# Own PSUM tiles in place of shared pairs, and four weight slots in place of three, in a spectral mixer with a gated feed-forward

## The chip, the cores and the metric

The kernel runs on one core of one Trainium2 chip. The metric is the device time of one execution in microseconds. The engines' names in profile lines: PE is the matrix engine (PEld its weight loads), DVE the vector engine, ACT the scalar engine, POOL the GpSimd engine, SP the engine that issues all DMAs of this kernel.

## What is computed

A token matrix `x` of 8192 x 448 goes through two residual branches, both modulated by a condition vector `c`:

```python
mod = silu(c) @ w_mod                      # six rows: sa, ca, ga, sb, cb, gb
h = layernorm(x) * (1 + ca) + sa
x = x + ga * A(h)                          # spectral part
h = layernorm(x) * (1 + cb) + sb
x = x + gb * ((gelu(h @ w_gate) * (h @ w_up)) @ w_down)     # feed-forward part

def A(h):                                  # per 4 blocks of 112 channels
    z = rfft(h, over the 8192 tokens)      # complex
    h1 = relu(z @ w1 + b1)                 # complex product, relu on both parts
    o = h1 @ w2 + b2                       # complex product
    o = softshrink(o, 0.01)
    return irfft(o)
```

`w_gate` and `w_up` are 448 x 1792, `w_down` is 1792 x 448. All inputs and outputs are float32.

## The kernel before

**Spectral part.** The transform over 8192 = 128 x 64 tokens is done in two stages of matrix products. A first stage loads `x`, takes the statistics of its rows and makes the 128-point transform (`dft_a`, `out_a`), storing its result `td` in DRAM. Then 32 *units* (16 groups of frequencies `bt`, two halves `h` of the channels) run through a software pipeline. `step(i)` works on several units at once: it fetches unit i+2 (`fetch_t`), makes the 64-point transform of unit i (`stage_s2`, tag `pa`), splits unit i+1 into a high and a low half-precision part (`split_t`), makes the second product of the block MLP with softshrink for unit i-2 (`stage_m2`, two halves p, tag `pc`), the first part of the inverse transform for unit i-3 (`stage_i1`, tag `pd`), and the first MLP product for unit i-1 (`stage_m1`, tag `pb`). Each of these writes PSUM with PE, reads it back with ACT and then DVE (a high part and the remainder), and calls `bank(tag, ...)` twice a unit, once for each half of its work. `drain` ends the pipeline.

Between the stages of a step stand *hooks* (`load`, `pe`, `act`, `dve`, `pool`): work of the feed-forward part that is done early. In steps 3 to 16 that is the norms of the weights (`squares`, `norms`, `down_max`, `down_sums`); in steps 17 to 31 the weights are turned into *forms*, sums and differences of weight blocks in two half-precision parts (`load_forms`, `form_sums`, `forms_hi`, `forms_lo`, `store_forms`), and the down weights are made ready (`load_d4`, `down_hi`, `down_lo`). A form is the weight operand of one of seven column groups t; it takes 23 blocks of 128 columns, `NWB`, in two precisions, and is kept in DRAM (`wsd`) in the parts that `WPARTS` lists.

**Feed-forward part.** The tokens are worked through in 32 chunks of 2 x 128. Per chunk there are 7 *periods*, one for each form, and then the down products:

- `period(u)` runs the gate and up products of form `torder[u]` in four groups of matmuls, `stage_a` and `stage_b` for u, `stage_c` for u-1, `stage_d` for u-2, into `sets[u % 3]`, a tile of two PSUM banks, with the reads by ACT and DVE (`seed`, `copy_b`, `joins`, `gel3`, `mult3`, `gel1`, `mult1`), sums on POOL (`sums`) and the split into two precisions (`quant_hi`, `quant_lo`) between them. `torder` runs through the seven forms forwards in one chunk and backwards in the next, so the forms still held in a slot at the turn aren't fetched again.
- after period `LA` = 2 of a chunk `phase` runs: the second stage of the inverse transform for chunk i+2 (`inverse`, `residual`), and then `down` for chunk i-1, which makes seven products (numbered 0 to 6) of 7 x 3 matmuls each. They go to `d0`, `d1` (the two banks of `pd`) and `f0`, `f1` (the two banks of the set that is free). Its last step stores the output.
- `extra` and `first` (for the first chunk) list what else is done at the end of a period: the split of the inverse transform's inputs (`split_v`, `split_g`), the token operand's sums and packing into `pkt` (`token_sums`, `pack_hi`, `pack_lo`) and its transposition by DMA into `nt` (`transposes`, 12 DMAs of 4 blocks a chunk).

The forms live in slots of SBUF: two that the spectral part fills, and one more. `plan_slots` gives each u a slot, taking the one whose last use is longest ago, and notes in `refill` which u is to be fetched into it. `after(u, part)` issues this fetch right where the slot's part was used last.

**What sets the order.** The program's order is the order on each engine (`manual_schedule`); the framework adds the waits, by tiles. All DMAs are issued by SP in program order, and a DMA that waits holds those behind it.

Of the kernel before, what the change touches and what calls it, by code (L numbers as in the profile page):

```python
# [19 lines left out]
D = 448  # L20
# [3 lines left out]
HC = 224  # L24
# [11 lines left out]
WPARTS = (12, 11)  # L36
# [11 lines left out]
def spectral_geglu(ctx, tc, x, w1, b1, w2, b2, wg, wu, wd, cvec, wmod, cf1, cs2, cmi, cgm, out):  # L48
# [26 lines left out]
    ident = cpool.tile([128, 128], F16, name="ident")  # L75
    make_identity(nc, ident)
# [249 lines left out]
    with ExitStack() as bctx:  # L326
# [593 lines left out]

        def load_g(i):
# [64 lines left out]
        at(31, "load", load_g, 0)  # L986
        at(31, "load", load_v0)
# [7 lines left out]

    with ExitStack() as cctx:
        cp = cctx.enter_context(tc.tile_pool(name="cp", bufs=1, side="right"))
        wslot.append(cp.tile([128, 2, NWB, 128], F16, name="ws2"))
        nch = NB // CB
        NT_ = nch * NP  # L1000
        sets = [banks2[tag] for tag in ("pa", "pb", "pc")]
        pdn = banks2["pd"]
# [6 lines left out]
        def plan_slots():  # L1009

            held = [[0 if wat[0] == s else 1, -1] for s in range(2)] + [[2, -1]]
# [11 lines left out]
        def load_part(u, part):  # L1023

            a, n = (0, WPARTS[0]), WPARTS
            lo = a[part]
            dma(slot_of[u][:, :, lo : lo + n[part]], wsd[part][torder[u]])

        def after(u, part):

            if u in refill:
                load_part(refill[u], part)
# [109 lines left out]
        def transposes(i, gs):  # L1142
            if i not in nts:
                nts[i] = cp.tile([128, 2, NXT, 128], F16, tag="nt", name="nt", bufs=2)
            for g in gs:
                sw_, c = divmod(g, NXT // 4)
                o = 64 * sw_ + 512 * c
                nc.sync.dma_start(nts[i][:, sw_, 4 * c : 4 * c + 4, :], pkt[:, o : o + 512], transpose=True)  # L1148
# [79 lines left out]
        def gel1(u):  # L1228
            gls[u] = cp.tile([128, 128], F32, tag="gl1", name="gl1", bufs=2)
# [39 lines left out]
        def down(i, pf, mid=lambda n: None):  # L1269
# [13 lines left out]
            d0, d1, f0, f1 = (p[:, b, :] for p in (pdn, pf) for b in range(2))  # L1283
            heads = [(0, d0), (1, d1)] + ([(2, f0), (4, f1)] if last else [])
# [16 lines left out]
            V.tensor_tensor(u2, product(i, f1, 4, rest if last else range(NP)), p1, ALU.add)  # L1301
            V.tensor_tensor(u4, product(i, d0, 3), u2, ALU.add)  # L1302
# [226 lines left out]
```

## Time and profile before

| | us |
|---|---|
| median of 3 runs | 2530.32 (2530.08 to 2536.79) |
| the profiled execution | 2528.75 |
| its span, first to last instruction | 2526.9 |

| part of the span | us from its start |
|---|---|
| first `stage_s2` matmul starts | 82.2 |
| last `stage_i1` first matmul starts | 777.6 |
| first `gel3` of the feed-forward part starts | 824.6 |
| end | 2526.9 |

How to read the lines that follow: a group's line holds the source line, engine, operation, `output<-inputs` by the program's tile names, shapes and count, then busy time and mean duration of one in ns, then the idle time of the engine ahead of it and who ended it (`<-`). A line of the table of waits holds engine and line, the releaser, the total in us, the number of times and the longest. A line of the timeline holds start and duration in us, engine, line, operation, count, and in brackets the idle time before. "issue" is time in which an engine waited for nothing that the profile shows. Matmuls overlap in the pipeline and their ends are modelled, so distances between starts say more than durations.

### The profile page before, as it was taken

Reading aid. Unit: us, or ns where it says so; the run is one execution under the profiler, and the core shown is the slowest. Engines: PE = TensorE matmul, PEld = TensorE weight load, DVE = VectorE, ACT = ScalarE, POOL = GpSimd, SP = SyncE. Lnnn points to the kernel's source line nnn. Section 1 sums busy time; section 2 is a strip of 40 time slices with the busy share of each in tenths; the row PEclk is TensorE's granted clock in tenths of the full one; section 3 lists DMA queues with packets and bytes.
Section 4 is the critical chain, followed back from the end, with each engine's and each line's share of the span. In section 5 each row is a group of like instructions: output and inputs, shape, how many; then the busy total and the mean of one; then the engine's idle time right before and its main releaser. Section 6 shows DMA issues by size and latency. Waiting matters only on the chain.

```text
span 2526.9 us, 92738 instructions
## 1 busy us (share of the span) xinstructions
PE 2034.0 (80%) x41348; PEld 1893.0 (75%) x41348; DVE 1459.9 (58%) x2958; ACT 1047.3 (41%) x1917; POOL 1107.1 (44%) x1531
## 2 busy tenths in 40 slices
PE   7676676655655798889888988989898898898898
PEld 3565666555554788888888888988888888888887
DVE  8423323444444576676666766767666766677644
ACT  6333333344431444443344443444334444344442
POOL 3122323232210555455455554655545555555532
PEclk9757657777777999999999999999999999999999
DMA  9643433335335977667866687666776766777562
GB/s 351 210 136 95 123 87 89 100 104 153 102 97 150 191 178 192 156 162 180 177 177 185 160 184 175 180 182 160 187 164 168 190 159 162 189 175 196 142 162 82
DMA packets 378984, 405.18 MB, mean 160 GB/s; under 512 B 223700, under 2 KB 287320, under 8 KB 378584
## 3 DMA queue, kind: packets, MB, share of 16 engines
q1 hardware_dynamic: 378584, 399.26, 60.9%
q8 instruction: 323, 5.29, 0.9%
q14 instruction: 77, 0.63, 0.1%
HBM read 290.96 MB, written 57.80 MB: 138 GB/s over the span
## 4 chain that ended last, share of the span: by engine, by line
PE 67%; DVE 13%; issue 7%; ACT 7%; DMA 3%; SPq 2%; POOL 1%; ACTq 0%; DVEq 0%; POOLq 0%
PE pb L1164 11%; PE pa L1164 11%; PE pc L1164 11%; PE pd L1264 4%; PE pd L1266 3%; PE pd L1265 3%; DVE y L470 2%; SPq L1148 1%; DVE x L1226 1%; ACT t L462 1%; PE pc L448 1%; PE pb L421 1%; PE pa L375 1%; ACT th L112 1%; DVE c L1210 1%
## 5 line engine op out<-in xcount | busy, mean ns | idle before, releaser
L1164 PEld LDWEIGHTS <-ws 64*128 64x128 f16 x33600 | 965.7, 95 | 197.6 <-issue 186.2
L1164 PE MATMUL pa<-nt,ws 64*128 64x128 f16 x11250 | 384.4, 219 | 64.0 <-issue 37.0
L1164 PE MATMUL pb<-nt,ws 64*128 64x128 f16 x11250 | 386.7, 219 | 51.5 <-issue 40.7
L1164 PE MATMUL pc<-nt,ws 64*128 64x128 f16 x11100 | 379.9, 218 | 50.4 <-issue 38.3
L1254 DVE SCALAR_TENSOR_TENSOR ac<-x,sa_act,ac 128x896 f16<-128x896 f32 x224 | 317.8, 1419 | 19.8 <-ACT ac L1245 19.8
L1222 ACT ACTIVATE gl<-c,dg 128x384 f32<-128x384 f32 x224 | 138.0, 616 | 400.8 <-DVE c L1216 385.8
L1264 PE MATMUL pd<-wd,ac 128*128 128x224 f16 x896 | 233.3, 260 | 30.2 <-DVE u L1302 15.4
L1266 PE MATMUL pd<-wd,ac 128*128 128x224 f16 x896 | 232.7, 260 | 1.8 <-DVE ac L1254 1.0
L1265 PE MATMUL pd<-wd,ac 128*128 128x224 f16 x896 | 232.7, 260 | 0.8 <-issue 0.8
L1245 ACT ACTIVATE ac<-x,sa_act 128x896 f16<-128x896 f32 x224 | 231.2, 1032 | 0.6 <-DVE x L1240 0.4
L1237 POOL TENSOR_TENSOR x<-x 128x128 f32<-128x128 f32 x223 | 105.6, 474 | 271.6 <-DVE x L1226 271.6
L470 DVE SCALAR_TENSOR_TENSOR y<-pc,t 64x224 f32<-64x224 f32 x256 | 99.5, 389 | 187.4 <-ACT t L462 184.8
L1226 DVE TENSOR_TENSOR x<-c,gl 128x384 f32<-128x384 f32 x224 | 181.6, 811 | 31.0 <-ACT gl L1222 31.0
L1265 PEld LDWEIGHTS <-ac 128*128 128x128 f16 x1568 | 153.6, 98 | 59.8 <-issue 59.6
L114 POOL TENSOR_TENSOR yl<-y,yh 128x448 fp32r<-128x448 f32 x63 | 73.7, 1170 | 268.8 <-ACT yh L112 268.8
L1308 POOL TENSOR_TENSOR o<-u,p 128x224 f32<-128x224 f32 x32 | 21.1, 659 | 383.8 <-DVE u L1307 383.8
L1264 PEld LDWEIGHTS <-ac 128*128 128x128 f16 x1568 | 153.6, 98 | 9.0 <-issue 7.9
L114 POOL TENSOR_TENSOR tl<-tr,th 128x896 f16<-128x896 f32 x30 | 56.5, 1883 | 227.4 <-ACT th L112 174.6
L1266 PEld LDWEIGHTS <-ac 128*128 128x128 f16 x1568 | 153.5, 98 | 2.7 <-DVE ac L1254 1.3
L448 PE MATMUL pc<-w2h,hh 113*128 113x224 f32 x128 | 52.6, 411 | 112.6 <-DVE y L470 112.6
L1240 POOL TENSOR_TENSOR x<-x 128x128 f32<-128x128 f32 x223 | 129.2, 579 | 19.2 <-DVE x L1233 18.9
L439 DVE SCALAR_TENSOR_TENSOR hl<-pb,hh 112x512 fp32r<-112x512 f32 x60 | 41.5, 692 | 144.5 <-ACT hh L438 144.3
(345 smaller groups left out, 4636.1 us busy)
## 6 DMA issues: line engine op xcount, KB each, us to landing
ws<-wsd SPq DMA_DIRECT2D x129, 768.0 KB, 5.9
ws<-wsd SPq DMA_DIRECT2D x129, 704.0 KB, 5.3
tr<-td SPq DMA_DIRECT2D x64, 224.0 KB, 4.0
vd<-us SPq DMA_DIRECT2D x64, 224.0 KB, 2.9
xx<-in_A_x SPq DMA_DIRECT2D x32, 448.0 KB, 4.3
v<-vd SPq DMA_DIRECT2D x63, 224.0 KB, 2.8
out<-x SPq DMA_DIRECT2D x31, 448.0 KB, 2.7
xt<-in_A_x SPq DMA_DIRECT2D x15, 896.0 KB, 13.2
```

The costliest lines, as they stand in the source:

```text
L114: (el or V).tensor_tensor(lo, src, h, ALU.subtract)
L470: V.scalar_tensor_tensor(y[ri * 64 : ri * 64 + 64, gi], pv[si, ri], LAM, tv[si, ri], op0=ALU.add, op1=ALU.min)
L1164: T.matmul(ps2[:, pr, reg * 128 : reg * 128 + 128], slot[rows, hl, wb + j, :], xblock(i, pr, xb + xo + j), start=start and j == 0 and m == ...
L1222: S.activation(gls[u], cts[u][:, 0], AF.Gelu_apprx_tanh, scale=dg)
L1226: V.tensor_tensor(xs[u][:, 1::3, :], cts.pop(u)[:, 1], gls.pop(u), ALU.mult)
L1237: e.tensor_tensor(s1, a21, a22, ALU.add)
L1240: e.tensor_tensor(s4, a12, s2, ALU.subtract)
L1245: S.activation(acts[u][:, 0], xs[u][:, 0:7], AF.Copy, scale=sa_act[:, t : t + 1])
L1254: V.scalar_tensor_tensor(acts[u][:, 1], xs.pop(u)[:, 0:7], sa_act[:, t : t + 1], acts[u][:, 0], op0=ALU.mult, op1=ALU.subtract)
L1264: T.matmul(ps, ac[:, 0, ka], w[:, 0, kb], start=n == 0, stop=False)
L1265: T.matmul(ps, ac[:, 0, ka], w[:, 1, kb], start=False, stop=False)
L1266: T.matmul(ps, ac[:, 1, ka], w[:, 0, kb], start=False, stop=n == NP - 1)
```

## The change

**PSUM.** In the spectral part the four tiles of two banks each (`banks2`, alternated by `turn`) become a pool of one-bank tiles: each call of `bank` takes a new tile, two buffers for each tag. That pool is closed before the feed-forward part, which opens another: three tiles of two banks as `sets`, and two tiles of one bank as `pdn`. In `down` product 4 now goes to `d0` and product 3 to `f1` (they were the other way round), and of the last chunk's products three in place of four are begun early.

**Slots.** There are four slots of forms, in three parts of 12, 6 and 5 blocks. `after` only notes a fetch in `pending`; `flush` issues what is noted, at the end of each period, ahead of that period's `extra`. To find the room in SBUF `gl1` has one buffer in place of two, and an identity that isn't used is no longer made.

**Order of the other DMAs.** `load_g(i+2)` moves from `phase` of the chunk before to the end of period 0, `load_v(i+3)` to the end of period 6, `split_v` from period 0 to period 1. The twelve transposes, which stood in periods 1 and 2 (4 and 8), are now spread over periods 1 to 4 (2, 6, 2, 2); those of the first two chunks take 12 blocks each in place of 4. The load of the modulation row `gb` moves from the feed-forward part's start into the last units of the spectral part.

```diff
-WPARTS = (12, 11)
+WPARTS = (12, 6, 5)
...
-    psum = ctx.enter_context(tc.tile_pool(name="psum", bufs=1, space=bass.MemoryType.PSUM))
-    banks2 = {tag: psum.tile([128, 2, 512], F32, name=tag) for tag in ("pa", "pb", "pc", "pd")}
-    turn = dict.fromkeys(banks2, 0)
+    pctx = ExitStack()
+    psum = pctx.enter_context(tc.tile_pool(name="psum", bufs=2, space=bass.MemoryType.PSUM))
 
     def bank(tag, name):
-        turn[tag] += 1
-        return banks2[tag][:, turn[tag] % 2, :]
+        return psum.tile([128, 512], F32, tag=tag, name=name)
...
+        def load_gb():
+
+            raw = fp.tile([128, 14, 128], F32, tag="wr", name="wr", bufs=2).rearrange("p k f -> p (k f)")
+            raws["gb"] = [raw[:112, h * 896 : (h + 1) * 896].rearrange("p (q c) -> p q c", q=4) for h in range(2)]
+            for h in range(2):
+                c0 = 5 * D + h * HC
+                dma(raws["gb"][h], wmod[:, c0 : c0 + HC].rearrange("(k p) c -> p k c", p=112))
...
+        at(31, "load", load_gb)
...
+    pctx.close()
...
-        wslot.append(cp.tile([128, 2, NWB, 128], F16, name="ws2"))
+        wslot += [cp.tile([128, 2, NWB, 128], F16, name=f"ws{s}") for s in (2, 3)]
...
-        sets = [banks2[tag] for tag in ("pa", "pb", "pc")]
-        pdn = banks2["pd"]
+        psum2 = cctx.enter_context(tc.tile_pool(name="psum2", bufs=1, space=bass.MemoryType.PSUM))
+        sets = [psum2.tile([128, 2, 512], F32, name=f"set{s}") for s in range(3)]
+        pdn = [psum2.tile([128, 512], F32, name=f"pdn{s}") for s in range(2)]
...
-                    s = min(range(3), key=lambda n: held[n][1])
+                    s = min(range(4), key=lambda n: held[n][1])
...
+        pending = []
+
         def after(u, part):
 
             if u in refill:
-                load_part(refill[u], part)
+                pending.append((refill[u], part))
+
+        def flush(keep=()):
+
+            for u, part in [p for p in pending if p[1] not in keep]:
+                load_part(u, part)
+                pending.remove((u, part))
...
-            gls[u] = cp.tile([128, 128], F32, tag="gl1", name="gl1", bufs=2)
+            gls[u] = cp.tile([128, 128], F32, tag="gl1", name="gl1")
...
-            d0, d1, f0, f1 = (p[:, b, :] for p in (pdn, pf) for b in range(2))
-            heads = [(0, d0), (1, d1)] + ([(2, f0), (4, f1)] if last else [])
+            (d0, d1), (f0, f1) = pdn, (pf[:, b, :] for b in range(2))
+            heads = [(0, d0), (1, d1)] + ([(2, f0)] if last else [])
...
-            V.tensor_tensor(u2, product(i, f1, 4, rest if last else range(NP)), p1, ALU.add)
-            V.tensor_tensor(u4, product(i, d0, 3), u2, ALU.add)
+            V.tensor_tensor(u2, product(i, d0, 4), p1, ALU.add)
+            V.tensor_tensor(u4, product(i, f1, 3), u2, ALU.add)
...
             on(u - 2, stage_d)
-            on(u - 2, lambda v: after(v, 1))
+            on(u - 2, lambda v: after(v, 2))
...
             on(u - 1, stage_c)
+            on(u - 1, lambda v: after(v, 1))
...
-                loads(j + 1)
...
         extra = {
-            0: [(2, split_v)],
-            1: [(2, split_g), (1, transposes, range(0, 4))],
-            2: [(1, transposes, range(4, 12))],
-            3: [(2, token_sums, 0), (2, pack_hi, [0]), (2, pack_lo, [0])],
-            4: [(2, token_sums, 1), (2, pack_hi, [1]), (2, pack_lo, [1])],
+            0: [(2, load_g)],
+            1: [(2, split_v), (2, split_g), (1, transposes, [0, 6])],
+            2: [(1, transposes, [1, 7, 11, 5, 2, 8])],
+            3: [(1, transposes, [3, 9]), (2, token_sums, 0), (2, pack_hi, [0]), (2, pack_lo, [0])],
+            4: [(1, transposes, [4, 10]), (2, token_sums, 1), (2, pack_hi, [1]), (2, pack_lo, [1])],
             5: [(2, pack_hi, [2]), (2, pack_lo, [2])],
-            6: [(2, pack_hi, [3]), (2, pack_lo, [3])],
+            6: [(2, pack_hi, [3]), (2, pack_lo, [3]), (3, load_v)],
         }
...
-            if i < nch and k == LA and i > 0:
-                for d, fn, *args in extra[k]:
-                    if i + d > 1 and i + d < nch:
-                        fn(i + d, *args)
+            if i == nch:
+                continue
+            flush()
+            for d, fn, *args in extra[k]:
+                if i + d > (1 if fn is transposes else 2) and i + d < nch:
+                    fn(i + d, *args)
+            if k == LA and i > 0:
                 phase(i)
-            elif i < nch:
-                for d, fn, *args in extra[k]:
-                    if i + d > (1 if fn is transposes else 2) and i + d < nch:
-                        fn(i + d, *args)
```

More of the change, by code (lines that the diff above doesn't have):

```diff
@@ L7 @@
 from concourse import mybir
-from concourse.masks import make_identity
 from concourse._compat import with_exitstack
@@ L1009, in plan_slots @@
         def plan_slots():
-            held = [[0 if wat[0] == s else 1, -1] for s in range(2)] + [[2, -1]]
+            held = [[0 if wat[0] == s else 1, -1] for s in range(2)] + [[2, -1], [3, -1]]
             for u, t in enumerate(torder):
@@ L1341, in loads @@
         def loads(j):
-            if j < nch:
-                load_v(j)
-                load_g(j)
+            load_v(j)
+            load_g(j)
         def phase(i):
@@ L1387, in spectral_geglu @@
         }
-        inverse(0, banks2["pa"], halves[0])
-        ga, gb = nxt[0]["ga"], bank("pd", "psm")
+        inverse(0, sets[0], halves[0])
+        ga, gb = pdn
         mod_half("ga", ga, 1)
@@ L1394, in spectral_geglu @@
         S.copy(ga_r[:, HC:], ga[:, HC:D])
[L1395 to L1400 removed]
+        inverse(0, sets[1], halves[1])
         for h in range(2):
@@ L1409, in spectral_geglu @@
         loads(1)
-        for part in range(2):
+        for part in range(len(WPARTS)):
             load_part(2, part)
@@ L1423, in spectral_geglu @@
         S.copy(gb_r, gb[:, :D])
-        transposes(0, range(12))
-        inverse(1, banks2["pb"])
+        transposes(0, range(4), 12)
+        for part in range(len(WPARTS)):
+            load_part(3, part)
+        inverse(1, sets[2])
         residual(1)
```

25 lines of the change are left out of this document (8 added, 17 removed).

## The prediction, made before the changed kernel was run

> **What bounds the kernel now.** I read the page first (sums, the slices, the chain that ended last), then windows cut at the program's own steps, then the table of waits and the timeline.
>
> ```profile
> span 2526.9 us, 92738 instructions
> ...
> PE 2034.0 (80%) x41348; PEld 1893.0 (75%) x41348; DVE 1459.9 (58%) x2958; ACT 1047.3 (41%) x1917; POOL 1107.1 (44%) x1531
> ...
> PEclk9757657777777999999999999999999999999999
> ...
> q8 instruction: 323, 5.29, 0.9%
> ...
> PE 67%; DVE 13%; issue 7%; ACT 7%; DMA 3%; SPq 2%; POOL 1%; ACTq 0%; DVEq 0%; POOLq 0%
> ```
>
> TensorE carries two thirds of the last chain. The clock row splits the span: about 0.7 of full speed over the first third (the spectral part), full speed afterwards (the feed-forward part). The next fence cuts the spectral part into its first five steps, steps 5 to 16, steps 17 to 30, and the rest; columns after the length are busy time of PE, PEld, DVE, ACT, POOL, then granted clock, DMA share, GB/s. The two rows below it are the same cuts for L375 alone, which issues 8 matmuls a step, so 96 and 112 are 12 and 14 steps.
>
> ```profile
> 82.00:159.00 77.00, 50.17 (x307) 45.70 (x307) 23.88 (x43) 25.41 (x42) 14.35 (x10) 0.66 0.57 176
> 159.00:417.40 258.40, 179.76 (x1073) 163.17 (x1072) 86.87 (x195) 91.90 (x149) 75.91 (x104) 0.66 0.35 99
> 417.40:725.20 307.80, 184.46 (x1097) 165.61 (x1096) 130.35 (x218) 121.59 (x186) 95.31 (x77) 0.72 0.44 117
> 725.20:778.30 53.10, 35.56 (x178) 31.49 (x177) 19.14 (x35) 17.65 (x30) 5.66 (x5) 0.74 0.19 51
> ```
>
> ```profile
> 159.00:417.40 258.40, 25.42 (x96) 17.18 (x96) 0.66 0.35 99
> 417.40:725.20 307.80, 23.99 (x112) 17.22 (x113) 0.72 0.44 117
> ```
>
> A step lasts 258.4/12 = 21.5 us in the first cut ("A") and 307.8/14 = 22.0 us in the second ("B"). In A it holds 15.0 us of PE, 7.2 of DVE, 7.7 of ACT, 6.3 of POOL and 0.35 x 21.5 = 7.5 us of DMA: nothing is full. In B: PE 13.2, DVE 9.3, ACT 8.7, POOL 6.8, DMA 9.7. What fills the rest are waits of PE:
>
> ```profile
> PE pc L448 <- DVE y L470: 112.6, 32, 6.1
> ...
> PE pb L421 <- DVE hl L439: 53.0, 28, 4.1
> ...
> PE pa L375 <- DVE zl L384: 45.5, 29, 1.6
> ...
> PE pd L500 <- ACT us L504: 19.9, 32, 0.7
> ```
>
> ```profile
> 361.06 0.41 PE L453 MATMUL pc<-w2h,hl 112*128 112x224 f32 x1
> 361.57 0.63 ACT L462 ACTIVATE t<-pc,nlam 128x448 f32<-128x448 f32 x1 [0.23 <-PE pc L453]
> 362.31 1.60 DVE L470 SCALAR_TENSOR_TENSOR y<-pc,t 64x224 f32<-64x224 f32 x4 [1.97 <-ACT t L462]
> 364.05 0.52 PE L448 MATMUL pc<-w2h,hh 113*128 113x224 f32 x1 [2.58 <-DVE y L470]
> ```
>
> The matmul at 364.05 writes the *other* half of `pc` than the one ACT and DVE are reading (`bank` alternates the index), yet it starts 0.14 us after the last read. So the two banks of one tile exclude each other, although nothing is shared. The four rows are this wait in four places, about once a step each: 231.0 us, 7.2 us a step. Two different tiles don't do this: here PE writes `pc` while ACT reads `pb`.
>
> ```profile
> 1212.12 0.85 PE L1164 MATMUL pc<-nt,ws 64*128 64x128 f16 x24
> 1212.34 0.58 ACT L1201 COPY sb<-pb 128x512 f32<-128x512 f32 x1 [0.19 <-PE pb L1164]
> ```
>
> **The change, part by part.**
>
> **1. Spectral part: each call gets its own one-bank tile, two per tag.** The 7.2 us a step go; a tile then waits only for the readers of its predecessor but one, which finished a step ago. What is late next? The clock matters too:
>
> ```profile
> 755.11 0.41 PE L453 MATMUL pc<-w2h,hl 112*128 112x224 f32 x1
> 755.32 0.41 PE L448 MATMUL pc<-w2h,hh 113*128 113x224 f32 x1
> ...
> 755.86 0.27 PE L451 MATMUL pc<-w2h,hh 112*128 112x224 f32 x1
> 755.97 0.27 PE L452 MATMUL pc<-w2l,hh 112*128 112x224 f32 x1
> ```
>
> The same matmul starts every 0.21 us, then every 0.11: half clock and full clock. PE's 15.0 us a step in A, at the granted 0.66, are 15.0 x 0.66 = 9.9 us at full clock; B's are 13.2 x 0.72 = 9.5. [...]
>
> Upper bound of a new step: only the idle goes, 21.5 - 7.2 = 14.3 (A) and 22.0 - 7.2 = 14.8 (B). Lower bound: the fullest resource, PE's 9.9 (A) and the DMA's 9.7 (B). A dependent loop remains, since the second MLP product of a step needs `hl` of the step before:
>
> ```profile
> L439 DVE SCALAR_TENSOR_TENSOR hl<-pb,hh 112x512 fp32r<-112x512 f32 x60 | 41.5, 692 | 144.5 <-ACT hh L438 144.3
> ```
>
> Six matmuls twice at 0.11 (1.3), relu 0.63, two `y` of 1.60, `hl` twice 0.69: 6.5 us, in B plus the weight-form work that sits ahead of `hl` on DVE (9.3 - 7.2 = 2.1 more). Both lie under the lower bounds, so I stay nearer to those: 11 us in A, 13 in B (four resources between 8.7 and 9.7 in order there, so more is lost between them). A: 258.4 - 132 = **-126** (bounds -87 to -140). B: 307.8 - 182 = **-126** (-101 to -172). The five first steps fill the pipeline beside a DMA that is busy 0.57 x 77 = 44 us: 77 to 57, **-20** (0 to -33). The drain has the same waits: **-10** (0 to -15).
>
> **2. Feed-forward part: `pd` becomes two tiles, and products 3 and 4 change places.** The down products show the same exclusion, three times a chunk, 32 chunks:
>
> ```profile
> 1200.50 0.26 PE L1265 MATMUL pb<-wd,ac 128*128 128x224 f16 x1
> 1200.59 0.26 PE L1266 MATMUL pb<-wd,ac 128*128 128x224 f16 x1
> 1201.29 0.26 PE L1264 MATMUL pb<-wd,ac 128*128 128x224 f16 x1 [0.43 <-ACT p L1298]
> ```
>
> ```profile
> PE pd L1264 <- DVE u L1302: 15.4, 32, 0.5
> PE pd L1264 <- ACT p L1292: 13.9, 32, 0.4
> ...
> PE pb L1264 <- ACT p L1298: 4.8, 11, 0.4
> ```
>
> Starts are 0.70 apart in place of 0.10, so 0.60 is lost where the idle column says 0.43: 0.17 more each. A chunk loses 0.48 + 0.43 + 0.43 + 3 x 0.17 = 1.85 us. After: product 1 goes to a tile of its own; product 4, on `pdn[0]`, stands between the two that share a tile, and its 21 matmuls at 0.10 cover the copy (0.43); product 5 has its own tile. 32 x 1.85 = **-59** (-40 to -59; PE is on the chain here). The last product keeps its real wait. With one head fewer in the last chunk at most 18 matmuls, 1.7 us, lose their cover: within rounding.
>
> **3. Four slots, three parts, flushed at the end of a period.** By the slot plan 3 forms a chunk are fetched in place of 4: of the 129 issues below some 98 stay.
>
> ```profile
> ws<-wsd SPq DMA_DIRECT2D x129, 768.0 KB, 5.9
> ```
>
> PE hardly ever waits for weights, so this is not where they cost. The instruction queue is: 5.29 MB for 2 x 41348 instructions are 64 B each, 323 packets of 256 instructions, and PE stops between such packets when other transfers run:
>
> ```profile
> 1219.00:1228.00 9.00, 4.60 (x160) 4.26 (x156) 6.35 (x11) 3.28 (x6) 5.01 (x10) 1.00 0.85 310
> 1228.00:1238.00 10.00, 9.83 (x354) 9.66 (x350) 5.43 (x10) 7.79 (x14) 5.74 (x10) 1.00 0.02 6
> ```
>
> ```profile
> PEld L1164 <- issue: 186.2, 205, 11.8
> ```
>
> At 310 GB/s PE is busy 4.60 of 9.00 us, at 6 GB/s 9.83 of 10.00. The 186.2 us (waits for nothing shown) are my bound for all such stops. Traffic beside the gate/up products per chunk now: three of four forms (4.4 MB at 768 + 704 KB), inputs and output (1.5), four of twelve transposes (0.5): 6.4 MB. After: three forms less the three parts flushed just ahead of the down products (2.9), the same 1.5, six transposes (0.8): 5.2, a fifth less. A fifth of 186 is 37; some of the rest now meets in one burst, so I take **-28** (+20 to -140). [...]
>
> **4. What moves closer to its use.** `load_g` goes from a chunk ahead to the end of period 0, behind a weight part; its split runs at the end of period 1, where `split_v` now stands too.
>
> ```profile
> 1236.75 2.09 POOL L114 TENSOR_TENSOR vl<-v,vh 128x896 fp32r<-128x896 f32 x1 [0.30 <-ACT vh L112]
> ...
> 1242.97 1.04 POOL L114 TENSOR_TENSOR gl<-g,gh 128x256 fp32r<-128x256 f32 x1
> ```
>
> ```profile
> 1246.10 0.36 PE L1054 MATMUL pc<-vh,gl 128*128 128x448 f32 x1
> ```
>
> With both behind POOL's sums of that period, `gl` ends at 1242.97 + 2.09 + 1.04 = 1246.1, just when PE needs it. And `g` stands behind a part that lands 5.9 us after its issue, in a period of about 4.2 (300 matmul and load instructions at the quiet window's 704 in 10 us): the cast `gh` can hold ACT 1 to 1.5 us, with the next period's `seed` behind it and PE's third group of that period behind `seed`. I take 0.6 us a chunk, **+18** (0 to +70). Transposes in periods 3 and 4 delay the next packing of the same part of `pkt`, which is one to two periods off: 0 while these periods cover them, else ACT or POOL is held as by the late `g`, another 0.6 us a chunk. The single `gl1` buffer waits for a multiply of the period before, done by then: 0, else one short multiply. The identity that is no longer built stood ahead of the first load's arrival: 0.
>
> **5. Entry.** Four slots filled ahead remove this, and the earlier `gb` load comes off the same queue: **-4** (0 to -12).
>
> ```profile
> 856.50 3.06 PE L1164 MATMUL pc<-nt,ws 64*128 64x128 f16 x54 [4.09 <-DMA ws<-wsd]
> ```
>
> **Sum.** -126 - 126 - 20 - 10 - 59 - 28 + 18 - 4 = -355, so a span of 2526.9 - 355 = 2172. The profiled run was 2528.75 us, 1.9 over its span, and the median of the runs shown is 2530.32, 1.6 above that: **2175 us**.
>
> **The rivals.**
>
> *Half clock stays.* PE without waits but at half clock: 24 matmuls of each MLP product at 0.21, and the rest, at least 13.2 to 15.0 busy in a step; take 15. A -78, B -98, fill and drain -25, feed-forward -73: 2256. For it: PE waits for others half of the time even then. Against: full-clock spacing already occurs between today's waits.
>
> *The tiles still wait.* If a one-bank tile is released only with its neighbour, part 1 is 0 and parts 2 to 5 leave -73: 2457. Against: `pc` beside `pb` above.
>
> *All instruction stops go.* Fetching during the down products frees the queue wholly: 140 in place of 28, time 2063.
>
> *Slower.* SP is one queue, in order. The refills now stand at a period's end, behind the output store, which waits for POOL, and behind earlier transposes. If the parts for periods 4 to 6 land after their matmuls are due, PE stops in every chunk. The cover of the last one is the down products plus three periods, about 16 + 12.6 us; if it were eaten and 15 us a chunk were lost, 32 x 15 = 480 against 355: 2655. It decides from 355/32 = 11 us a chunk. Against: the refill is issued ahead of the transposes.
>
> **How the numbers follow.** Forecast 0.67, half clock 0.14, tiles still wait 0.07, all stops gone 0.09, slower 0.03. The forecast's bounds are about 2100 to 2270; 2085 to 2320 takes in half clock and leaves the last three out. What a measurement can't tell from no change is 0.3%, 7.6 us. All but the slower case are faster by more: 0.96 faster; 0.01 within, where late refills just cancel the gain; 0.03 slower.
>
> **What would show it.** Right: the waits of L448 on `y`, L421 on `hl`, L375 on `zl`, L1264 on `u` and `p` gone from the table; L375's starts 10 to 13 us apart a step; granted clock over 0.85 in that part; feed-forward entered some 280 us earlier; some 98 weight issues a part; L1164's issue waits about 150 us. Wrong: step time over 14 us with clock 0.7 (half clock); new PE waits on `gl` or `seed` over 1 us a chunk; LDWEIGHTS waiting for `ws` from DMA (slower). A gain of the size forecast but at an unchanged spectral part would refute part 1.

## The result and the profile after

| | before | after |
|---|---|---|
| median of 4 runs, us | 2532.54 (2530.08 to 2536.79) | 2097.66 (2090.31 to 2106.23) |
| ratio, 95% interval | | 0.8283 (0.8242 to 0.8323) |
| the profiled execution, us | 2528.75 | 2103.25 |
| its span, us | 2526.9 | 2101.4 |

The page of the changed kernel, the same lines as before the change:

```profile
span 2101.4 us, 93045 instructions
...
PE 1871.1 (89%) x41348; PEld 1781.5 (85%) x41348; DVE 1479.4 (70%) x2958; ACT 1029.4 (49%) x1917; POOL 1116.5 (53%) x1529
...
PEclk9899988979999999999999999999999999999999
...
q8 instruction: 323, 5.29, 1.1%
...
PE 69%; DVE 17%; issue 6%; DMA 3%; ACT 2%; SPq 2%; POOL 0%; ACTq 0%; DVEq 0%; POOLq 0%
...
ws<-wsd SPq DMA_DIRECT2D x98, 768.0 KB, 5.5
ws<-wsd SPq DMA_DIRECT2D x98, 384.0 KB, 5.6
ws<-wsd SPq DMA_DIRECT2D x98, 320.0 KB
```

The same 41348 matmuls as before, in 163 us less of PE busy time. The first third of the clock row now stands near full speed. Each weight part has 98 issues, where it had 129. On the chain that ended last ACT fell from 7% to 2%, and PE and DVE took its place.

The windows of the changed kernel, cut at the same steps as before (first five steps, 5 to 16, 17 to 30, the rest), columns as in the prediction:

```profile
81.20:118.50 37.30, 34.26 (x307) 33.18 (x307) 22.74 (x42) 24.08 (x41) 13.36 (x10) 0.84 0.95 303
118.50:227.50 109.00, 108.29 (x1074) 104.90 (x1072) 84.05 (x195) 87.08 (x150) 75.44 (x101) 1.00 0.86 248
227.50:394.70 167.20, 134.42 (x1097) 129.60 (x1096) 128.80 (x215) 117.97 (x186) 103.60 (x80) 0.88 0.78 212
394.70:427.20 32.50, 26.14 (x176) 25.25 (x176) 23.87 (x40) 17.45 (x31) 8.14 (x6) 0.84 0.59 149
```

In steps 5 to 16 PE is busy 108.29 of 109.00 us at a clock of 1.00: PE alone sets the time there, 9.1 us a step. In steps 17 to 30 (11.9 us a step) PE, DVE and the DMA are each between 0.77 and 0.80 full and none sets it alone. In the first five steps the DMA is busy 0.95 of the time.

The waits of the changed kernel. L1177 is the gate and up matmul (L1164 before), L445 a matmul of the second MLP product that reads `hl`:

```profile
PEld L1177 <- issue: 167.0, 210, 4.8
...
PE set L1177 <- issue: 100.7, 107, 4.1
...
ACT gh L107 <- DMA g<-cgm: 29.5, 29, 3.2
...
POOL pk L1153 <- DMA nt<-pk: 28.1, 18, 2.9
...
PE pm L445 <- DVE hl L434: 24.0, 9, 4.1
...
PE set L1177 <- DVE c L1229: 17.3, 25, 1.6
```

Of the four waits of about 231 us in all, 6.4 us are left (one wait of 2.5 us on `y`, one of 3.9 us on `hl` in the first MLP product). The longest of PE's waits in the spectral part is now the true dependence on `hl`, the row of L445. Two waits on DMAs are new, `gh` on `g` and `pk` on the transposes. The issue waits, 186.2 us before, are still 167.0.

Two places of the timeline of the changed kernel, where the exclusion was to be seen before. The first is the border between two halves of the second MLP product, the second the border between down products 2 and 4:

```profile
130.04 0.27 PE L448 MATMUL pm<-w2h,hl 112*128 112x224 f32 x1
130.15 0.27 PE L443 MATMUL pm<-w2h,hh 113*128 113x224 f32 x1
...
131.34 1.15 ACT L457 ACTIVATE t<-pm,nlam 128x448 f32<-128x448 f32 x2
```

```profile
1192.39 0.26 PE L1279 MATMUL set<-wd,ac 128*128 128x224 f16 x1
1192.49 0.26 PE L1277 MATMUL pdn<-wd,ac 128*128 128x224 f16 x1
```

The second half starts 0.11 us after the first, ahead of the read of either; the next down product 0.10 us after the last. Both borders cost 0.6 us or more before.

Where the 425.5 us of span went, by the starts of the same instructions in both traces ("a chunk" is the mean of 30; its down stretch runs from the first matmul of its down products to the first gate/up weight load behind them, its gate/up stretch from there to the next chunk's first down product):

| stretch | before | after | difference | predicted |
|---|---|---|---|---|
| first five steps | 77.0 | 37.3 | -39.7 | -20 |
| steps 5 to 16 | 258.4 | 109.0 | -149.4 | -126 |
| steps 17 to 30 | 307.7 | 167.2 | -140.5 | -126 |
| drain | 52.3 | 32.4 | -19.9 | -10 |
| entry, last `stage_i1` to first down product | 100.1 | 87.7 | -12.4 | -4 |
| the 31 chunks that follow | 1625.8 | 1564.6 | -61.2 | -69 |
| of it a down stretch | 16.16 | 14.28 | -1.88 a chunk | -1.85 |
| of it a gate/up stretch | 36.68 | 36.68 | 0.00 a chunk | -0.3 |
| ahead of the first step, and tail | 105.3 | 103.1 | -2.2 | 0 |

So the surprise is in two places: the spectral part gained a quarter more than forecast, and the gate and up products gained nothing, though a quarter of the weight fetches is gone.

### The profile page after: what moved, and what is told of

The parts are those of the page before. It is cut to its first block, busy times and chain, and to the rows that moved or that the text cites. A ratio compares the mean times of both kernels' runs of the same rounds, so it can differ in the third digit from the quotient of the medians.

```text
span 2101.4 us, 93045 instructions
## 1 busy us (share of the span) xinstructions
PE 1871.1 (89%) x41348; PEld 1781.5 (85%) x41348; DVE 1479.4 (70%) x2958; ACT 1029.4 (49%) x1917; POOL 1116.5 (53%) x1529
## 3 DMA queue, kind: packets, MB, share of 16 engines
q8 instruction: 323, 5.29, 1.1%
## 4 chain that ended last, share of the span: by engine, by line
PE 69%; DVE 17%; issue 6%; DMA 3%; ACT 2%; SPq 2%; POOL 0%; ACTq 0%; DVEq 0%; POOLq 0%
PE set L1177 35%; PE pdn L1277 4%; PE pdn L1279 4%; PE pdn L1278 4%; PE set L1279 3%; PE set L1277 3%; PE set L1278 3%; DVE x L1239 3%; DVE c L1223 2%; DVE ac L1267 2%; PE ps L204 2%; DVE y L465 1%; DVE c L1229 1%; DVE tf L1127 1%; DMA g<-cgm 1%
## 5 line engine op out<-in xcount | busy, mean ns | idle before, releaser
L1177 PE MATMUL set<-nt,ws 64*128 64x128 f16 x33600 | 996.5, 218 | 147.9 <-issue 100.7
L1177 PEld LDWEIGHTS <-ws 64*128 64x128 f16 x33600 | 968.0, 95 | 176.9 <-issue 167.0
L1223 DVE TENSOR_TENSOR c<-set,sb 128x512 f32<-128x512 f32 x224 | 153.6, 686 | 120.4 <-PE set L1177 111.6
L1277 PE MATMUL pdn<-wd,ac 128*128 128x224 f16 x896 | 233.6, 261 | 1.1 <-issue 0.6
L1279 PE MATMUL pdn<-wd,ac 128*128 128x224 f16 x896 | 233.1, 260 | 1.2 <-DVE ac L1267 1.2
L1278 PE MATMUL pdn<-wd,ac 128*128 128x224 f16 x896 | 233.1, 260 | 0.0
L1250 POOL TENSOR_TENSOR x<-x 128x128 f32<-128x128 f32 x223 | 106.0, 475 | 221.6 <-DVE x L1239 221.6
L1239 DVE TENSOR_TENSOR x<-c,gl 128x384 f32<-128x384 f32 x224 | 198.9, 888 | 28.2 <-ACT gl L1235 28.0
L1214 ACT COPY sb<-set 128x512 f32<-128x512 f32 x224 | 129.8, 580 | 102.7 <-PE set L1177 102.4
L1277 PE MATMUL set<-wd,ac 128*128 128x224 f16 x672 | 174.0, 259 | 0.1
L1279 PE MATMUL set<-wd,ac 128*128 128x224 f16 x672 | 174.0, 259 | 0.0
L1278 PE MATMUL set<-wd,ac 128*128 128x224 f16 x672 | 174.0, 259 | 0.0
L465 DVE SCALAR_TENSOR_TENSOR y<-pm,t 64x224 f32<-64x224 f32 x256 | 99.5, 389 | 59.6 <-ACT t L457 55.9
L1246 DVE TENSOR_TENSOR x<-set,gl 128x128 f32<-128x128 f32 x224 | 63.9, 285 | 94.5 <-ACT gl L1243 94.1
L109 POOL TENSOR_TENSOR yl<-y,yh 128x448 fp32r<-128x448 f32 x63 | 81.1, 1287 | 92.3 <-ACT yh L107 74.1
```

The costliest lines, as they stand in the source:

```text
L465: V.scalar_tensor_tensor(y[ri * 64 : ri * 64 + 64, gi], pv[si, ri], LAM, tv[si, ri], op0=ALU.add, op1=ALU.min)
L1177: T.matmul(ps2[:, pr, reg * 128 : reg * 128 + 128], slot[rows, hl, wb + j, :], xblock(i, pr, xb + xo + j), start=start and j == 0 and m == ...
L1214: S.copy(sbs[u], sets[u % 3][:, :, 0:256])
L1223: V.tensor_tensor(c[:, :, 1:3, :], p[:, :, 0:256].rearrange("p g (r c) -> p g r c", r=2), b[:, :, 0:128].rearrange("p g (o c) -> p g o c", ...
L1239: V.tensor_tensor(xs[u][:, 1::3, :], cts.pop(u)[:, 1], gls.pop(u), ALU.mult)
L1250: e.tensor_tensor(s1, a21, a22, ALU.add)
```

## The experiments

**Which part of the change brings what.** The first two kernels add to the kernel before: the rotating tiles alone, then the down products' own tiles. The third and fourth take from the kernel after: one buffer for each tag, so that the halves wait for each other again though every tile is a single bank; and the same with matmuls into a spare bank that fill the waits, which separates the clock from the waits.

```diff
 # e1, on the kernel before
-        turn[tag] += 1
-        return banks2[tag][:, turn[tag] % 2, :]
+        return psum.tile([128, 512], F32, tag=tag, name=name)
...
+        sets = [psum2.tile([128, 2, 512], F32, name=f"set{s}") for s in range(3)]
+        pdn = psum2.tile([128, 2, 512], F32, name="pdn")
 # e2, on e1
-        pdn = psum2.tile([128, 2, 512], F32, name="pdn")
+        pdn = [psum2.tile([128, 512], F32, name=f"pdn{s}") for s in range(2)]
...
-            V.tensor_tensor(u2, product(i, f1, 4, rest if last else range(NP)), p1, ALU.add)
-            V.tensor_tensor(u4, product(i, d0, 3), u2, ALU.add)
+            V.tensor_tensor(u2, product(i, d0, 4), p1, ALU.add)
+            V.tensor_tensor(u4, product(i, f1, 3), u2, ALU.add)
 # e3, on the kernel after, ahead of the first step; bank takes its tiles from the last of pools
+        pctx.close()
+        pools.append(pctx.enter_context(tc.tile_pool(name="psum1", bufs=1, space=bass.MemoryType.PSUM)))
 # e4, on e3: fill(5) between the halves of stage_s2 and stage_m1, fill(9) in stage_m2, fill(2) in stage_i1
+        def fill(n):
+            for _ in range(n):
+                T.matmul(spare, filled[:, 0:128], filled, start=True, stop=True)
```

> The kernel before with one-bank tiles, two per tag, in the spectral part alone; the feed-forward part keeps four pairs, three slots and its order. Theory (two banks of one tile exclude each other; without that PE also keeps full clock): the whole spectral gain of the changed kernel, some 350 us, so about 2182 us, steps of 9 us in A and 12 in B, clock near 1.0 in A. Rival (only the 231 us of listed waits go, the rest comes from the other parts of the change): about 2300 us.

> The same, and in the feed-forward part the two banks of the down products as tiles of their own, with products 3 and 4 changed about. Theory: 59 us less than the run with the spectral tiles alone, about 2123 us, down products 14.2 us in place of 16.0 a chunk, gate and up products unchanged at some 37 us. Rival (what the down products save is waited for afterwards, by later instruction blocks or late packing): within 10 us of the run with the spectral tiles alone. What then still separates it from the changed kernel (2098) is what slots, flush and moved loads are worth, about 12 us of entry and 0 to 15 of the rest.

> The changed kernel with one buffer per tag in the unit loop of the spectral part. Theory (a pair in one tile is worth no more than one bank): the spectral part as slow as before, steps of 21 to 22 us, clock about 0.7, about 2098 + 350 = 2448 us. Rival (the pair let part of the work overlap): slower than that, 2500 us or more.

> As the run with one buffer, and PE runs extra matmuls into a spare bank (2 to 9 of 128x512 at each of the four places of a step where it waits, 20 to 21 a unit, 4.5 us at full clock); their results are not used. Theory (the waits also cost because they lower the clock): PE keeps full clock, its own work falls from 15 to about 9 us a step, and the run is some 120 us faster than with one buffer alone, about 2320 us, although it computes more. Rival (the clock only follows and costs nothing): no faster, 2448 to 2590 us.

| kernel | us | ratio to before (95%) | steps 5 to 16 | steps 17 to 30 | down, a chunk | gate/up, a chunk |
|---|---|---|---|---|---|---|
| e1, rotating tiles alone | 2161.11 | 0.8538 (0.8499 to 0.8576) | 109.0 | 165.5 | 16.21 | 36.35 |
| e2, and the down tiles | 2101.55 | 0.8307 (0.8266 to 0.8347) | 109.0 | 167.4 | 14.20 | 36.21 |
| after | 2097.66 | 0.8283 (0.8242 to 0.8323) | 109.0 | 167.2 | 14.28 | 36.68 |
| e3, after with one buffer | 2462.64 | 0.9733 (0.9685 to 0.978) | 262.1 | 314.4 | 14.47 | 36.40 |
| e4, e3 with fillers | 2364.15 | 0.9351 (0.9317 to 0.9386) | 214.2 | 288.3 | 14.53 | 36.54 |

The two tile changes together (2101.55) can't be told from the whole change (2097.66). The rotating tiles are worth 370 us on the kernel before (2531.17 in those runs) and 365 us within the kernel after (e3), the down tiles 60 us on e1. All the rest, slots, parts, flush and moved loads, is worth about 4 us as a whole, less than the intervals.

The windows of e3 over steps 5 to 16 and 17 to 30, and its waits:

```profile
157.40:419.50 262.10, 183.37 (x1073) 166.29 (x1071) 86.91 (x195) 91.89 (x149) 75.88 (x104) 0.64 0.35 98
419.50:733.90 314.40, 193.20 (x1097) 174.49 (x1096) 131.23 (x218) 121.56 (x186) 95.84 (x77) 0.70 0.42 115
```

```profile
PE pm L443 <- DVE y L465: 109.1, 32, 6.1
...
PE pm L416 <- DVE hl L434: 54.0, 28, 4.1
...
PE ps L370 <- DVE zl L379: 45.6, 29, 1.6
...
PE pi L495 <- ACT us L499: 20.1, 32, 0.7
```

These are the rows of the kernel before to within 3.5 us each (109.1 + 54.0 + 45.6 + 20.1 = 228.8 us, where it had 231.0), and the clock is back at 0.64 and 0.70. So two banks in one tile behaved as a single buffer: that settles what the timeline was read to say.

The same windows of e4:

```profile
146.80:361.00 214.20, 176.15 (x1324) 130.37 (x1324) 86.91 (x195) 90.06 (x149) 76.05 (x104) 0.98 0.43 122
361.00:649.30 288.30, 220.03 (x1390) 161.89 (x1389) 132.49 (x218) 121.02 (x186) 95.45 (x77) 0.88 0.47 125
```

PE does 251 and 293 matmuls more there, yet the stretches are 47.9 and 26.1 us shorter, with the clock at 0.98 and 0.88. The waits between the halves are still in the program. So the clock is worth at least 98 us (2462.64 to 2364.15) of the 365 by itself: the fillers' own time is already paid in this, and with them the clock of steps 17 to 30 is still only 0.88. The gain was expected at about 120. The other 267 us hold what the waits cost beyond the clock, the fillers' time and the rest of the clock's share, which these runs don't separate.

**Why the gate and up stretch did not get shorter.** Three causes were on the table: the traffic that remains, the late `g`, and where in the chunk the refills run. e5 issues none of the refills of the chunks. e6 issues `load_g` two periods earlier. e7 holds back what the first two periods of a chunk have noted until the end of period 2, so that it leaves just ahead of the inverse transform and the down products; e8 is both.

```diff
 # e5, on the kernel after
             for u, part in [p for p in pending if p[1] not in keep]:
-                load_part(u, part)
                 pending.remove((u, part))
 # e6, on the kernel after
-            0: [(2, load_g)],
+            0: [],
...
-            5: [(2, pack_hi, [2]), (2, pack_lo, [2])],
+            5: [(2, pack_hi, [2]), (2, pack_lo, [2]), (3, load_g)],
 # e7, on the kernel after; e8 is e6 and e7
-            flush()
+            if k >= LA:
+                flush()
```

> The changed kernel without the fetches into freed slots: later forms are computed with whatever a slot holds (work left out: 96 of 98 form transfers). Theory (PE stops at the edges of its instruction packets because other transfers are under way): of 5.2 MB a chunk beside the gate and up products 2.3 stay, so the issue waits of those products' weight loads fall from 148 to about 65 us and the run to about 2030 us. Rival (the stops come with the rate of instructions and transfers don't matter): issue waits unchanged, 2090 to 2100 us.

> The changed kernel with load_g moved from the end of period 0 to the end of period 5 of the chunk before. Theory (the late g holds ACT, and seed and PE behind it): the 28 us of ACT waiting for g go, PE's waits on DVE c and ACT set fall by half, 8 to 20 us less: about 2084 us. Rival (it is hidden): 2098 us, within 3.

> The changed kernel with the flush held back in periods 0 and 1, so that six of a chunk's nine weight parts (3.4 MB) are issued together just ahead of the down products. Theory (transfers beside gate and up products cost stops): 1.9 of 5.2 MB leave that stretch, issue waits 148 to about 95, some 35 to 50 us less: about 2055 us. Rival (it takes its place elsewhere: transposes queue behind six transfers, the packing waits for them, or weights come late): 2095 us or more, with POOL pk waiting for DMA nt over 28 us or PE for ws.

> Both, the held flush and the early g. Theory: the two gains add, about 2040 us. Rival (g's transfer, now in period 5, costs as many stops as it saves waits): no better than the held flush alone.

| kernel | us | ratio to before (95%) | gate/up, a chunk | `set` waiting for issue, in the chunks |
|---|---|---|---|---|
| after | 2097.66 | 0.8283 (0.8242 to 0.8323) | 36.68 | 93.8 |
| e5, no refills | 1986.67 | 0.7834 (0.7796 to 0.7873) | 33.20 | 15.5 |
| e6, early `g` | 2105.99 | 0.8308 (0.8265 to 0.8351) | 36.58 | 101.2 |
| e7, refills held | 2036.55 | 0.8033 (0.7989 to 0.8077) | 34.78 | 59.9 |
| e8, held and early `g` | 2048.1 | 0.808 (0.8041 to 0.8119) | 35.16 | 71.9 |

e5 gains 111 us, more than was expected of the refills: PE hardly stops, though the edit takes none of its instructions away. One gate and up stretch of the kernel before, of after, of e5 and of e7, each a row of its windows:

```profile
1527.40:1566.60 39.20, 32.76 (x1056) 31.12 (x1055) 26.47 (x41) 22.01 (x41) 24.63 (x38) 0.98 0.62 175
```

```profile
1201.10:1236.00 34.90, 31.68 (x1056) 30.58 (x1055) 26.36 (x41) 22.01 (x41) 25.59 (x38) 1.00 0.69 151
```

```profile
1144.10:1176.60 32.50, 31.42 (x1056) 30.50 (x1055) 28.14 (x41) 21.88 (x41) 24.79 (x36) 1.00 0.42 80
```

```profile
1163.70:1199.00 35.30, 31.55 (x1056) 30.54 (x1055) 27.01 (x41) 22.07 (x41) 24.23 (x36) 1.00 0.59 118
```

The 1056 matmuls keep PE busy for 31.4 to 31.7 us in the last three, and the rest of a stretch is PE standing. The last number times the length is the traffic: 6.9, 5.3, 2.6 and 4.2 MB. Single stretches differ from the means of the table by up to 2.5 us, so the traffic is better taken over all 30: length times GB/s gives a mean of 6.25 MB a stretch before, 5.56 after, 2.63 in e5 and 4.38 in e7. Beside the gate and up products it thus fell by 11%, not by the fifth of the forecast (6.4 to 5.2 MB), and the DMA share of these stretches even rose from 0.59 to 0.66. The stops fell in the same measure as the bytes, and most of what PE won there it lost again: its own waits for issue in the chunks fell from 113.1 to 93.8 us, but those for readers (`c`, `seed`, `o`) rose from 20.1 to 31.7 us and those in the inverse transform from 1.1 to 5.4 us. That the place counts shows in e7: all refills are still made (157 GB/s over 400 us, against 152 in the kernel after), they only run beside other matmuls, and 61 us go. The timeline of the kernel after shows why the place may count:

```profile
1211.38 3.77 PE L1177 MATMUL set<-nt,ws 64*128 64x128 f16 x128 [0.71 <-issue]
1215.94 11.24 PE L1177 MATMUL set<-nt,ws 64*128 64x128 f16 x384 [0.80 <-issue]
1227.45 3.75 PE L1177 MATMUL set<-nt,ws 64*128 64x128 f16 x128 [0.27 <-issue]
```

The stops stand after 128 matmuls or three times 128. With a weight load each that is one packet of 256 instructions, the size that the prediction took from the instruction queue. Such a packet lasts 3.75 us here. Down matmuls start 0.10 us apart, so 128 of them last over 12 us. That the fetch of a packet is held up by other transfers, and beside the down products has that much longer to come in, is the author's explanation, which no run shows by itself; that the stops get fewer and shorter is measured:

```profile
PEld L1176 <- issue: 64.4, 136, 1.5
```

```profile
PEld L1177 <- issue: 111.8, 190, 1.7
```

These are e5 and e7 in the table of waits, within the chunks; the kernel before had 164.6 us there and the kernel after 147.6.

In e6 ACT's wait for `g` is gone from its table and the time is not lower (2105.99, with an interval that overlaps that of the kernel after). That alone doesn't tell whether the late `g` costs nothing or whether its earlier place costs as much: the gate and up stretch of e6 is 0.10 us a chunk shorter, the down stretch 0.37 longer, and in e7 no wait for `g` is listed in the first place, yet e8 is no faster than e7. PE's waits decide: for `c` and `seed`, which the late `g` can hold, PE waits 16.8 us in the chunks of the kernel after and 13.4 in those of e6. So the late `g` costs some 3 us, and what waits for it has time.

**Where the moved loads and transposes belong.** e9 is e7 with the inputs' loads back at `phase`, at the start of the down products, as in the kernel before; e10 is e7 with the transposes as 4 DMAs of 12 blocks, all just ahead of the down products. e11 is e2 with a fourth slot alone (and, for its room, one buffer of `gl1` and no identity): two parts, fetched at once, loads and transposes where they were before the change. e12 is the kernel after without `flush`: each part is fetched at once.

```diff
 # e9, on e7
-            0: [(2, load_g)],
+            0: [],
...
-            6: [(2, pack_hi, [3]), (2, pack_lo, [3]), (3, load_v)],
+            6: [(2, pack_hi, [3]), (2, pack_lo, [3])],
...
+                if j + 1 < nch:
+                    loads(j + 1)
 # e10, on e7
-            1: [(2, split_v), (2, split_g), (1, transposes, [0, 6])],
-            2: [(1, transposes, [1, 7, 11, 5, 2, 8])],
+            1: [(2, split_v), (2, split_g)],
+            2: [(1, transposes, [0, 2, 3, 1], 12)],
 # e11, on e2
+        wslot += [cp.tile([128, 2, NWB, 128], F16, name=f"ws{s}") for s in (2, 3)]
-                    s = min(range(3), key=lambda n: held[n][1])
+                    s = min(range(4), key=lambda n: held[n][1])
 # e12, on the kernel after
-                pending.append((refill[u], part))
+                load_part(refill[u], part)
```

> The kernel with the held flush, and load_v and load_g back in phase, behind the held weight parts and the transposes, so that their 1.0 MB also moves into the down products. Theory (what counts is how much is transferred beside gate and up products): 3.3 MB become 2.3 as in the run without refills, 20 to 35 us less than 2037: about 2010 us. Rival (14 us of down products are too short for 3.4 + 1.0 MB and six transposes, the rest runs into the next period in one burst): 2037 us or more.

> The kernel with the held flush and the chunk's transposes as four DMAs of 12 blocks at the end of period 2, behind the held parts, in place of twelve of 4 over four periods. Theory (a transpose costs SP mostly per DMA: at the entry 12 took 20.1 us and 4 wide ones 9.7): none is left beside gate and up products but what runs over, POOL's 40 us of waiting for nt goes, 5 to 25 us less: about 2022 us. Rival (the wide ones land too late behind 3.4 MB, the packing of period 3 waits and with it ACT): 2037 us or more.

> The kernel with all tiles (2101.6 us) and four slots in place of three, in two parts fetched where they are freed; no flush, and the moved loads and transposes as before. Theory (less traffic is fewer stops, and the changed kernel gave this back by its flush and its moves): issue waits under 131 us, 20 to 40 us less, about 2072 us. Rival (the fourth slot itself is worth nothing): 2095 to 2105 us.

> The changed kernel with each fetch issued where its part is freed, not at the period's end; the rest as changed. Theory (the flush puts several parts and g into one burst, which costs stops): 8 to 20 us less than 2098, about 2084 us. Rival (when within a period they are issued does not matter, and the moved loads and transposes are the cost): 2098 us, within 4.

| kernel | us | ratio to before (95%) | gate/up, a chunk | the 31 chunks | MB beside a chunk's gate/up |
|---|---|---|---|---|---|
| e2, three slots | 2101.55 | 0.8307 (0.8266 to 0.8347) | 36.21 | 1550.1 | 6.48 |
| e11, four slots alone | 2054.14 | 0.8114 (0.807 to 0.8157) | 34.81 | 1506.3 | 4.96 |
| e12, after without flush | 2091.21 | 0.8273 (0.8224 to 0.8322) | 36.25 | 1553.9 | 5.59 |
| after | 2097.66 | 0.8283 (0.8242 to 0.8323) | 36.68 | 1564.6 | 5.56 |
| e7, after, held | 2036.55 | 0.8033 (0.7989 to 0.8077) | 34.78 | 1504.9 | 4.38 |
| e10, held, wide transposes | 2032.06 | 0.8028 (0.7992 to 0.8064) | 34.54 | 1498.6 | 4.94 |
| e9, held, loads in down | 2020.7 | 0.7992 (0.7961 to 0.8024) | 34.22 | 1489.9 | 4.18 |

e11 settles the question: the fourth slot by itself is worth 47 us on e2, so the loss of traffic does pay, and the kernel after gives that gain back. e12 says where not: without `flush` the time is the same within the intervals. Between e12 and e11 lie the three parts in place of two and the moved loads and transposes, 37 us, outside both intervals. In e12 as in the kernel after, 0.6 MB more passes beside the gate and up products than in e11. Which of these weighs most isn't settled. e9 against e7 has 16 us for the loads' place, with intervals that just overlap; e10 against e7 has 4.5 us, too little to tell, though POOL's wait for `nt` is gone from its table. The part count was not tried by itself; e10, with three parts, stands as well as e11 with two (34.54 and 34.81 us a stretch, 4.94 and 4.96 MB), which speaks against it as the main cause. Nor are bytes the whole of it: e2 has more of them than the kernel after and a shorter stretch.

The issue rows in the chunks of e11, of e12 and of e9 go with the times:

```profile
PEld L1161 <- issue: 106.9, 151, 2.5
```

```profile
PEld L1177 <- issue: 140.7, 188, 3.2
```

```profile
PEld L1177 <- issue: 91.6, 155, 2.1
```

e9 is the fastest of these kernels that leaves no work out: 2020.7 us, 77 us below the changed kernel and a fifth below the one before.

## Why the prediction was right, and where its sum was off

The forecast of 2175 us was of the right kind and 77 us too high; 2097.66 lies within the range, below the likeliest case's own bounds by a hair (about 2100). By the number alone the rival in which all instruction stops go (2063) is nearer. It is out by its mechanism: 147.6 us of stops are left in the chunks, and 67 of the 77 us lie in the spectral part.

**The bound and the four waits: right.** The waits named are gone but for 6.4 us and with them the half clock. e3 brings both back by the buffer alone (228.8 us of waits, clock 0.64 and 0.70).

**Part 1, mechanism right, size too small.** The sum of its four terms was -282 and measured -350. A step was put at 11 and 13 us and takes 9.1 and 11.9. The step that failed is "so I stay nearer to those: 11 us in A". In A the lower bound itself (15.0 x 0.66 = 9.9 us) was above the truth: PE's measured 108.29/12 = 9.0 us a step leaves no loss between the resources at all, and why busy time times the mean clock came out 0.9 us too high stays open. In B the step lies 2.2 us above the bound of 9.7. Three of the four terms, all but B's, lie outside their own bounds. The dependent loop through `hl` shows in nine waits of 24.0 us in all in the second product, not in every step. The first five steps had a lower bound of -33, that is 44 us of DMA; after the change the DMA is busy 0.95 x 37.3 = 35 us there and moves 303 x 37.3 = 11.3 MB, where it moved 176 x 77 = 13.6 MB at a lower rate: neither its busy time nor what falls into that stretch was fixed.

**The clock: right.** That PE holds full clock once the waits are gone, on which the 9.9 us of part 1 leans, was the author's estimate: the run of the kernel before does not show it in the spectral part. The later runs do in steps 5 to 16: without the waits the clock there is 1.00, and with the waits left in and only their gaps filled e4's goes from 0.64 to 0.98. In steps 17 to 30 it came to 0.88 in both. The rival of a half clock that stays is out by the 1.00 and 0.88 of the kernel after, and that of tiles that still wait by the waits that are gone.

**Part 2: right.** -59 forecast; 1.88 us a chunk is 31 x 1.88 = -58 in the table above, and e1 to e2 gives -60 by itself.

**Part 3, the step that failed is "5.2, a fifth less. A fifth of 186 is 37".** The traffic there fell by 11%, to 5.56 MB, and the stops with it, from 164.6 to 147.6 us; what PE won by that it lost to the waits for readers and in the inverse transform, so the stretch kept its 36.68 us. e11 shows that a fourth slot with the old order takes 6.48 MB to 4.96 and brings 47 us (44 of them in the chunks), more than the 28 forecast; parts and new order together took it back. That two errors, a slot worth more and moves that cost more, left a sum near the forecast's is luck. The "about 150 us" of issue waits that the prediction asked for came out at 167.0 over the run. Of the rival in which all stops go, e5 shows the size: about 111 us, by leaving all refills out, not by fetching them during the down products. That the stops go with the other transfers is measured: 64.4 us of them without refills against 147.6 with, for the same PE instructions.

**Part 4, wrong in its mechanism.** "the cast `gh` can hold ACT" came true (29 waits, 29.5 us), but PE lost only some 3 us by it, by its waits in e6, so most of the +18 was not on the path. That transposes in periods 3 and 4 delay a packing came true as well (18 waits, 28.1 us); e10 has none of these waits and is 4.5 us below e7, within the intervals. What the moves cost is most likely their traffic beside the gate and up products (5.56 MB, where e11 has 4.96), which the prediction counted as "the same 1.5, six transposes (0.8)".

**Part 5: too small.** -12.4 in place of -4. On SP the transposes of the first chunk, first in the kernel before and then after:

```profile
791.80 20.11 SPq L1148 DMA_TRANSPOSE nt<-pk  x12
```

```profile
442.55 9.67 SPq L1161 DMA_TRANSPOSE nt<-pk  x4
```

Four DMAs of 12 blocks held the queue 10.4 us less than twelve of 4. The section on the change names this edit; the prediction gave it no term. The entry of e2, with neither slot nor wide transposes, is 101.8 us long, that of e11, with the slot, 94.8, and that of the kernel after 87.7; in single executions, that gives about 7 us to the slot and as much to transposes and `gb` load.

**The slower rival** never came near: the table of the kernel after has no wait of PE for weights, and in the chunks the refills land in time even when e7 holds them back to the end of period 2.

## What to carry to other kernels

Give a buffer that is to be written while its neighbour is read a tile of its own: indexing halves of one tile serialized them here (365 us within the kernel after, by e3), and the trace showed it as a matmul that started 0.14 us after the last read of the other half. When waits on a dense engine go and the granted clock was low, put the new step near the fullest resource at full clock: both gains came together here (6.4 us left of 231 us of waits, clock 0.66 to 1.00 and 0.72 to 0.88), and one stretch reached that bound (9.1 us a step against 9.9 forecast) while the other stayed above it (11.9 against 9.7). Less traffic paid 47 us here with the loads and transposes left in their places (e11), and about 4 where they moved too (the kernel after, against e2): try DMAs that are not urgent beside products whose matmuls start further apart (0.10 us in the down products against 0.03 in the gate and up products; e7 gained 61 us by it), and measure traffic in the stretch where it hurts, over many of its repeats, not over the run and not in one.

## What the runs showed of the hardware

- Matmuls into a bank that nobody reads shortened the program (2364.15 us in e4, 2462.64 in e3). In e4 steps 5 to 16 hold 1324 matmuls in place of 1073 and take 214.2 us in place of 262.1, with the granted clock at 0.98 in place of 0.64.
- PE's stops for issue changed with the kernel's own transfers. On the gate and up weights they were 164.6 us in the chunks before, 147.6 after, 111.8 with the refills moved (e7), 91.6 with the input loads moved too (e9) and 64.4 without refills (e5). The matmuls were the same: 33600 in the run before and after, and none changed by the edits of e5, e7 and e9. Before and after, the instruction queue moved 323 packets, 5.29 MB. That its fetches compete with the other transfers is the author's reading.
- Fewer and wider DMA transposes held their queue for less time: 48 blocks took 20.11 us as twelve DMAs (1.68 each) and 9.67 us as four (2.42 each), the two rows above. Over the whole run of the kernel before the median DMA of 4 blocks took 1.27 us. How the cost splits between DMA and block is open: an estimate from the two rows, if it is linear, gives 1.3 us a DMA and 0.09 a block.
